# A long fused kernel on one core: taps copied straight from a row in SBUF, and a new order of the first loads, decodes and splits

## The chip, the cores and the metric

The kernel runs on 1 core of a Trainium2 chip. The metric is device time in microseconds (us) of one execution, the median of several runs; lower is better. Three runs of the kernel before took 1014.91, 1015.44 and 1015.61 us.

## The reference, cut to what matters

Three stages on x of shape (4, 4224, 192), everything float32. `weight` is 8 x 7, `U` is 4224 x 32, `V` is 32 x 4224, and each of the two MLPs has `w_ch1` of 192 x 768 and `w_ch2` of 768 x 192.

```python
# 1. causal convolution along the sequence: 7 taps (a softmax over weight), 8 heads of 24 channels
w = softmax(weight, axis=-1)
x = einsum('hk,bskhg->bshg', w, windows_of_7(x))
# 2. low-rank mixing along the sequence, then an MLP
u = x + ((x^T @ U) @ V)^T
x = u + relu(u @ w_ch1) @ w_ch2
# 3. real part of a 2-D Fourier transform, a normalization, then a second MLP
u = x + real(fft(fft(x, axis=1), axis=2))
out = u + relu(normalize(u) @ w_ch1') @ w_ch2'
```

On the host only the layout is changed; `U`, `V` and the MLP weights arrive as pairs of 32-bit words (float64 bits), which the kernel turns into float32 itself.

## The kernel before, in words

**Units of work.** The sequence of a batch is cut into 11 blocks of 384 rows. There are 88 block passes: 44 through the first MLP (stage 0), 44 through the second (stage 1). A pass has four pieces. The preparation (`pre1` for stage 0) adds the low-rank term to a block, takes its row sizes, makes the reciprocal scales (`scales`: tiles `cmax`, `rc`), splits the scaled block into a high and a low float16 part (`high` on ScalarE, `low` on GpSimd), and transposes both through a DMA into tile `ch`. `layer1` has six units, one per 128 hidden features: five matmuls of 384 columns, then an eviction by ScalarE (`hh`, line 650) and one by VectorE (`hl`, line 651). `layer2` has three units of 18 matmuls, closed by line 704; the result is stored to the DRAM tensor `x2d`.

**The start.** Before the first pass the kernel must make the first batch's convolution. `weight` is turned into taps on one partition (lines 983 to 989, tile `rowt`). The convolution's matrices are 64 shifted copies of that row per half of the partitions (tile `tap`); the row goes to the DRAM tensor `rowd` (lines 965, 966, 991) and comes back from there in two DMAs (line 995). x arrives in three chunks per batch (`load_x`, tiles `xw`, three buffers); the first two have 128 x 2688 floats, the third 128 x 1920. Each chunk is convolved by PE (line 398, 16 matmuls per pair of heads), evicted in place by ScalarE (line 404), stored to DRAM as `x1d` (line 368) and multiplied with U (`gunit`, line 414). After the third chunk the 32 x 192 product is replicated (`gfin`: matmul `gr`, tile `grep`), which every stage-0 block of batch 0 needs (line 522, tile `h`; added on VectorE by line 525).

**Decoding.** `decode` turns two words into one float32 with five VectorE instructions of up to 384 columns: line 172 takes off the sign bit, 175 clamps, 176 shifts, 178 and 179 put the words together. A decoded MLP weight also gets a largest value (line 223, tile `mx`). From `mx` the scale comes through a matmul (`all_max`, tile `am`, line 121), and then the weights are split into float16 high and low parts (`split1h`, `split1e`, `split1a`, `split1b` for the first layer, `split2` for the second; lines 257 and 264). The first MLP's raw weights arrive in three parts: `wa`, `wb` (first layer) and `wc` (second layer).

**What sets the order.** Everything is issued in program order, engine by engine; SP issues nearly all DMAs, in order, and an SP instruction that waits holds up all behind it. The order of the start is a table of strings, `START`: a letter with a number runs so many units of a queue (`c` first batch's convolution, `d` the second's, `w` the first MLP's weights, `a` and `b` the preparation of blocks 0 and 1, `z` later pieces of V, `e` the split of V). Other names are single jobs: `X`, `Y` load chunks of batch 0 and 1, `P` parts of the weights, `U1`, `V`, `V12` parts of U and V, `u`, `v0` decode them, `A0` and `s` store chunks of `x1d` (`A0` the first 448 rows), `L` loads a block, `S` loads `sel`, `B0` and `B1` are matmuls on zeros that give PE something to do (18 and 44 of them, `AGAIN`), after 52 at the very start (`WARM`). The first string runs before block 0; string t runs after two units of layer 1, three strings to a block. The table `windows` places the second MLP's weights and all else over later steps.

## Time and profile before

| | |
|---|---|
| runs | 1014.91, 1015.44, 1015.61 us (median 1015.44) |
| span of the profiled execution | 1017.3 us, 1.9 us above the median; no other time is listed for it |
| PE busy | 979.1 us, 96% of the span |
| VectorE, ScalarE, GpSimd busy | 748.4, 604.4, 380.9 us |
| HBM | 61.69 MB read, 46.11 MB written |

PE (TensorE) is busy nearly all the time, so what can be won or lost lies in the stretches in which it waits, or in which its granted clock is below 1.00. The page's busy shares are means over the whole span; the first 130 us differ from the rest, so the views that matter are those by stretch: the windows (busy time, granted clock and DMA rate of each stretch), the timeline (single instructions, with the idle time before them and what ended it) and the waits. A row of the windows has the stretch, its length, then for PE, weight loads (PEld), VectorE (DVE), ScalarE (ACT) and GpSimd (POOL) the busy us and the instructions that begin in it, then PE's granted clock, the DMA engines' share and GB/s. A row of the timeline has start and length in us (of a merged run, from its first start to its last end), engine, line, instruction, tiles, sizes and count, and in brackets the idle time just before.

### The profile page before, as it was taken

How to read it: one execution, taken by the hardware profiler on the slowest of the kernel's cores; microseconds unless marked ns; L12 is line 12 of the kernel's file. 1: busy time of each engine (PE TensorE's matmuls, PEld its weight loads, DVE VectorE, ACT ScalarE, POOL GpSimd, SP SyncE). 2: the span in 40 equal slices, each digit the busy share in tenths (PEclk: the TensorE clock that was granted, in tenths of full speed). 3: DMA queues.
4: the chain of work that ended last, by engine and by line, in shares of the span. 5: the costliest groups of instructions: out<-in, count | busy, mean ns of one | idle time of the engine just before them, and what ended most of it. 6: DMA issues, size and time to landing. Idle time of an engine off the chain costs nothing.

```text
span 1017.3 us, 25682 instructions
## 1 busy us (share of the span) xinstructions
PE 979.1 (96%) x9929; PEld 764.8 (75%) x9929; DVE 748.4 (74%) x2094; ACT 604.4 (59%) x1512; POOL 380.9 (37%) x397
## 2 busy tenths in 40 slices
PE   8789898999899999999999999998999999999998
PEld 5466676777677777877778887776888877877776
DVE  7766577689876656687776777897789787766663
ACT  2556554765676666656576666655656665555552
POOL 0111111253552344265534445564157651562110
PEclk9999999999999999999999999999999999999999
DMA  7596857685536666443425455433344332542332
GB/s 288 155 230 183 252 148 189 178 213 158 151 99 154 203 201 179 114 138 101 102 73 146 134 155 139 108 87 82 87 131 110 107 87 65 137 110 68 82 72 63
DMA packets 190804, 139.28 MB, mean 137 GB/s; under 512 B 128186, under 2 KB 164257, under 8 KB 189913
## 3 DMA queue, kind: packets, MB, share of 16 engines
q1 hardware_dynamic: 183095, 124.59, 45.6%
q0 software_dynamic: 7104, 12.70, 4.8%
q8 instruction: 77, 1.26, 0.5%
q14 instruction: 46, 0.38, 0.1%
q10 hardware_dynamic: 482, 0.35, 0.1%
HBM read 61.69 MB, written 46.11 MB: 106 GB/s over the span
## 4 chain that ended last, share of the span: by engine, by line
PE 62%; DVE 12%; DMA 11%; POOL 5%; issue 5%; ACT 4%; SPq 0%; DVEq 0%; ACTq 0%; POOLq 0%
PE l L665 24%; PE l L697 9%; PE l L701 8%; PE l L699 8%; PE l L655 5%; DMA ch<-sp 4%; DVE hl L651 3%; DMA xm<-x2d,mrow 2%; POOL xm L756 2%; PE cv L398 2%; PE sd L863 2%; PE s L879 2%; DMA x1d<-xw 1%; DVE x L790 1%; POOL xp L804 1%
## 5 line engine op out<-in xcount | busy, mean ns | idle before, releaser
L665 PE MATMUL l<-ch,w1h 128*128 128x384 f16 x1584 | 407.2, 327 | 15.4 <-DMA ch<-sp 10.1
L697 PE MATMUL l<-w2h,hh 128*128 128x192 f16 x1584 | 391.9, 247 | 5.8 <-DVE hl L651 4.5
L699 PE MATMUL l<-w2l,hh 128*128 128x192 f16 x1584 | 391.4, 247 | 1.2 <-DVE w2l L264 1.2
L701 PE MATMUL l<-w2h,hl 128*128 128x192 f16 x1584 | 391.4, 247 | 0.5 <-DVE hl L651 0.4
L651 DVE SCALAR_TENSOR_TENSOR hl<-l,hh 128x384 f16<-128x384 f32 x528 | 267.6, 549 | 127.2 <-ACT hh L650 126.1
L650 ACT ACTIVATE hh<-l 128x384 f16<-128x384 f32 x528 | 235.3, 494 | 155.7 <-PE l L655 155.3
L665 PEld LDWEIGHTS <-w1h 128*128 128x128 f16 x1584 | 155.1, 98 | 106.8 <-DMA ch<-sp 12.3
L697 PEld LDWEIGHTS <-hh 128*128 128x128 f16 x1584 | 155.6, 98 | 23.1 <-issue 12.3
L665 PE MATMUL l<-ch,w1l 128*128 128x384 f16 x528 | 172.7, 327 | 0.0
L699 PEld LDWEIGHTS <-hh 128*128 128x128 f16 x1584 | 155.7, 98 | 17.1 <-issue 6.5
L701 PEld LDWEIGHTS <-hl 128*128 128x128 f16 x1584 | 155.7, 98 | 3.1 <-DVE hl L651 1.4
L561 POOL TENSOR_TENSOR sp<-un,sp 128x576 f16<-128x576 f32 x44 | 57.3, 1302 | 250.4 <-ACT sp L578 228.3
L655 PE MATMUL l<-ch,w1l 128*128 128x384 f16 (+1 forms) x528 | 133.9, 327 | 0.0
L756 POOL DMA_INDIRECT xm<-x2d,mrow x84 | 84.9, 1011 | 21.3 <-issue 17.8
L631 POOL TENSOR_TENSOR sp<-un,sp 128x576 f16<-128x576 f32 x34 | 44.9, 1320 | 120.2 <-ACT sp L578 118.9
L625 ACT ACTIVATE un<-u,mr,rs 128x192 f32<-128x192 f32 x132 | 62.4, 537 | 25.3 <-DVE mr L619 24.7
L555 ACT ACTIVATE un<-u,rc 128x192 f32<-128x192 f32 x132 | 50.2, 445 | 43.0 <-DVE rc L550 43.0
L704 DVE SCALAR_TENSOR_TENSOR u<-l,cmax,u 128x192 f32<-128x192 f32 x132 | 54.5, 413 | 25.5 <-PE l L701 20.9
L665 PEld LDWEIGHTS <-w1l 128*128 128x128 f16 x528 | 51.8, 98 | 28.0 <-issue 4.0
L543 ACT ACTIVATE junk<-u 128x192 f16<-128x192 f32 x132 | 47.7, 361 | 40.6 <-DVE u L534 24.2
L849 POOL DMA_INDIRECT u<-x2d,mrow x64 | 62.4, 975 | 15.3 <-issue 11.7
L704 DVE SCALAR_TENSOR_TENSOR u<-l,ws,u 128x192 f32<-128x192 f32 x132 | 53.9, 410 | 18.2 <-PE l L701 18.0
(136 smaller groups left out, 1189.5 us busy)
## 6 DMA issues: line engine op xcount, KB each, us to landing
x2d<-u SPq DMA_DIRECT2D x68, 288.0 KB
u<-x1d SPq DMA_DIRECT2D x44, 288.0 KB
out_d<-u SPq DMA_DIRECT2D x43, 288.0 KB
x1d<-xw SPq DMA_DIRECT2D x36, 210.0 KB
u<-x2d SPq DMA_DIRECT2D x32, 192.0 KB
x<-x2d SPq DMA_DIRECT2D x60, 99.0 KB
xw<-x_d SPq DMA_DIRECT2D x4, 1344.0 KB
xw<-x_d SPq DMA_DIRECT2D x8, 672.0 KB
```

The costliest lines, as they stand in the source:

```text
L561: low_engine(0, b, j).tensor_tensor(out=sp[:, :, D:2 * D], in0=k["un"], in1=sp[:, :, :D], op=ALU.subtract)
L625: nc.scalar.activation(un[:, t], u[:, t], AF.Identity, scale=k["r"][:, t:t + 1], bias=k["m"][:, t:t + 1])
L650: nc.scalar.activation(hh[:, m], acc[m], AF.Relu)
L651: nc.vector.scalar_tensor_tensor(out=hl[:, m], in0=acc[m], scalar=0.0, in1=hh[:, m], op0=ALU.max, op1=ALU.subtract)
L655: nc.tensor.matmul(acc[m].rearrange("p (r n) -> p r n", r=TB), lhsT=w["l1"][rows, n, m * P:(m + 1) * P], rhs=kd[x][rows], start=False, sto ...
L665: nc.tensor.matmul(o, lhsT=w[v][:, e, ms], rhs=kd[x], start=(n == 0), stop=False)
L697: nc.tensor.matmul(o, lhsT=hh[:, m, rs], rhs=w["h2"][:, m], start=(m == 0), stop=False)
L699: nc.tensor.matmul(o, lhsT=hh[:, m, rs], rhs=w["l2"][:, m], start=False, stop=False)
L701: nc.tensor.matmul(o, lhsT=hl[:, m, rs], rhs=w["h2"][:, m], start=False, stop=(m == NM - 1))
L704: nc.vector.scalar_tensor_tensor(out=u[:, r], in0=o, scalar=sc, in1=u[:, r], op0=ALU.mult, op1=ALU.add)
L756: nc.gpsimd.indirect_dma_start(out=xs[c][1][:, g], out_offset=None, in_=x2d[b][:], in_offset=bass.IndirectOffsetOnAxis(ap=mrow[:99, k:k + ...
L849: nc.gpsimd.indirect_dma_start(out=u2[:, s0 + 2 * e], out_offset=None, in_=src[:], in_offset=bass.IndirectOffsetOnAxis(ap=mrow[:, k2 + e - ...
```

## The change

The taps no longer pass through DRAM: one VectorE memset clears a longer row, and two DMAs read the 64 shifted copies from that one row, which lies on one SBUF partition. `decode` has a new argument: for U's two halves and the first layer's weights (`wa`, `wb`) ScalarE takes the sign off by an Abs, instead of line 172 on VectorE; the scratch tile `dec` has two buffers. The order of loads, decodes, scales and splits in `START` is another, the matmuls on zeros are 34, 20 and 44, the store `A0` is issued by SP instead of ScalarE, and `split1a` stands ahead of `split1e`.

```diff
-WARM = 52
-AGAIN = (18, 44)
+WARM = 34
+AGAIN = (20, 44)
...
-        def decode(raw, out):
+        def decode(raw, out, first=False):
...
-            t = wrk.tile([P, DN], I32, name="dec", bufs=1)[:p, :n]
+            t = wrk.tile([P, DN], I32, name="dec", bufs=2)[:p, :n]
             g, h = nc.vector.tensor_scalar, nc.vector.scalar_tensor_tensor
-            g(out=t, in0=hi, scalar1=0x7FFFFFFF, scalar2=None, op0=ALU.bitwise_and)
-
             f = t.bitcast(F32)
+            if first:
+                nc.scalar.activation(f, hi.bitcast(F32), AF.Abs)
+            else:
+                g(out=t, in0=hi, scalar1=0x7FFFFFFF, scalar2=None, op0=ALU.bitwise_and)
...
-                decode(st["raw"][:, a:z], st["w"][:, a:z])
+                decode(st["raw"][:, a:z], st["w"][:, a:z], i == 0 and z <= FF + FH)
...
-                                       lambda: scaled(0, FF + FH, 0), split1h, split1e, split1a, split1b] + \
+                                       lambda: scaled(0, FF + FH, 0), split1h, split1a, split1e, split1b] + \
...
-        rowt = wrk.tile([1, KC * H], F32, name="hh", tag="hh")
+        rowt = wrk.tile([1, (2 * KC - 1) * H], F32, name="hh", tag="hh")
...
-        part(0)
+        load_x(0, 0)
         load_uv("u", 0, UH)
-        zer = wrk.tile([1, KC * H], F32, name="hl", tag="hl")
-        nc.vector.memset(zer, 0.0)
-        nc.scalar.dma_start(rowd[:, :nz], zer[:, :nz])
-        nc.scalar.dma_start(rowd[:, KC * H:], zer[:, :(KC - 1) * H])
+        nc.vector.memset(rowt, 0.0)
...
-        nc.sync.dma_start(rowd[:, nz:KC * H], rowt[:, nz:])
-
-        load_x(0, 0)
         for i in range(2):
-            nc.sync.dma_start(tap[KC * i:KC * i + KC].rearrange("p o h -> p (o h)"), bass.AP(
-                tensor=rowd.tensor, offset=rowd.offset, ap=[[H, KC], [1, KC * H]]))
+            nc.sync.dma_start(
+                tap[KC * i:KC * i + KC].rearrange("p o h -> p (o h)"),
+                bass.AP(tensor=rowt.tensor, offset=rowt.offset,
+                        ap=[list(rowt.ap[0]), [H, KC], [1, KC * H]]))
+        part(0)
...
-            decode(uv["u"][:, sl], uf[:, sl])
+            decode(uv["u"][:, sl], uf[:, sl], True)
...
-                    s0=lambda: stores[0](0, FIRST), A0=lambda: stores[0](0, 0, FIRST, nc.scalar))
+                    s0=lambda: stores[0](0, FIRST), A0=lambda: stores[0](0, 0, FIRST),
+                    L0=lambda: pre_load(0, 0))
...
-            "S U1 P1 X1 X2 V w2 u0 c4 B0 A0 L0 s0 L1 P2 u1 w c5 w3 v0 c4 w c3 w2 a4 w a4 b2 B1 w b4 w L2 b2 w",
-            "w s1", "", "w2 L3 V12", "w s2", "Y0", "z", "", "z", "d", "d Y1", "d", "d z", "d", "d z", "d Y2", "d e", "d", "d e", "d e",
+            "X1 U1 X2 S u0 w2 c4 A0 V P1 B0 L0 s0 P2 u1 c5 L1 s1 Y0 v0 c4 w c2 w3 c w a3 w a5 w2 B1 b4 w b4 w L2 w",
+            "w2", "", "w2 L3 V12", "s2", "Y1", "z", "", "z", "d", "d", "d z", "d", "d z Y2", "d", "d e", "d", "d e", "d", "d e",
```

Three places show how the instructions now stand (the lines of the code move by one or two). The first is VectorE behind the first layer's weights: `w1h` and `w1l` are their split parts, `cmax` and `rc` a block's scales, `u<-h,u` the low-rank addition (to block 0 first, then to block 1), `dec<-u` the first step of decoding `wc`. Before:

```order
L287 COPY w1h_90<-w1h_90 64x768
L525 TENSOR_TENSOR u<-h,u 128x192 x3
L294 COPY w1h_90<-w1h_90 64x384
L264 SCALAR_TENSOR_TENSOR w1l_91<-u_89,sc_370,w1h_90 64x384
L294 COPY w1h_90<-w1h_90 64x384
L264 SCALAR_TENSOR_TENSOR w1l_91<-u_89,sc_370,w1h_90 64x384
L296 COPY w1l_91<-w1l_91 64x768
L547 TENSOR_SCALAR cmax<-cmax 128x3
L550 RECIPROCAL rc<-cmax 128x3
L525 TENSOR_TENSOR u<-h,u 128x192 x3
L172 TENSOR_SCALAR dec<-u_89 128x384
```

And now:

```order
L287 COPY w1h_89<-w1h_89 64x768
L288 COPY w1h_89<-w1h_89 64x768
L548 TENSOR_SCALAR cmax<-cmax 128x3
L551 RECIPROCAL rc<-cmax 128x3
L295 COPY w1h_89<-w1h_89 64x384
L265 SCALAR_TENSOR_TENSOR w1l_90<-u_88,sc_435,w1h_89 64x384
L295 COPY w1h_89<-w1h_89 64x384
L265 SCALAR_TENSOR_TENSOR w1l_90<-u_88,sc_435,w1h_89 64x384
L297 COPY w1l_90<-w1l_90 64x768
L526 TENSOR_TENSOR u<-h,u 128x192 x3
L175 TENSOR_SCALAR dec<-u_88 128x384
```

Block 0's scales stand ahead of the split's last five instructions, no more behind them; block 0's addition, which stood among the splits, is now ahead of them all (just before these rows). Block 1's addition stands directly ahead of `wc`'s decoding in both.

The second is PE in block 0's layer 1, where `am` takes the largest value of `wc` to all partitions. `l_648` is the last of the six units before, `l_677` the first of block 1. Before:

```order
L655 LDWEIGHTS w1l_91
L655 MATMUL l_648<-ch,w1l_91 128x384
L121 MATMUL am<-sel,mx_94 128x128
L665 LDWEIGHTS w1h_90
L665 MATMUL l_677<-ch,w1h_90 128x384
L665 LDWEIGHTS w1l_91
L665 MATMUL l_677<-ch,w1l_91 128x384
```

And now, where `l_583` is block 0's second unit, `l_610` its third, and `h` the low-rank matmuls of block 2:

```order
L656 LDWEIGHTS w1l_90
L656 MATMUL l_583<-ch,w1l_90 128x384
L120 MATMUL am<-sel,mx_93 128x128
L523 MATMUL h<-grep,vt 128x192 x3
L666 LDWEIGHTS w1h_89
L666 MATMUL l_610<-ch,w1h_89 128x384
```

Four units of block 0 that stood ahead of `am` stand behind it. The 44 matmuls on zeros, which followed the `h` of blocks 0 and 1, now stand between the two.

The third is SP in block 4 (strings 13 to 15 and on), where batch 1's last chunk of x (`xw<-x_d` with 1920) goes past stores of its first chunk, and then the second MLP's first weights are loaded (`u_..<-wa_d`). Before:

```order
L585 DMA_TRANSPOSE ch<-sp 128x12x128
L504 DMA u<-x1d_66 128x576
L368 DMA x1d_67<-xw 56x5x192 x4
L368 DMA x1d_67<-xw 56x4x192 x2
L159 DMA xw<-x_d 128x1920
L716 DMA x2d_70<-u 128x576 x2
L585 DMA_TRANSPOSE ch<-sp 128x12x128
L504 DMA u<-x1d_66 128x576
L201 DMA u_1474<-wa_d 128x1536
```

And now:

```order
L586 DMA_TRANSPOSE ch<-sp 128x12x128
L505 DMA u<-x1d_66 128x576
L369 DMA x1d_67<-xw 56x5x192 x2
L158 DMA xw<-x_d 128x1920
L369 DMA x1d_67<-xw 56x5x192 x2
L369 DMA x1d_67<-xw 56x4x192 x2
L717 DMA x2d_70<-u 128x576 x2
L586 DMA_TRANSPOSE ch<-sp 128x12x128
L505 DMA u<-x1d_66 128x576
L202 DMA u_1453<-wa_d 128x1536
```

The load of the chunk stands ahead of four of the six stores `x1d<-xw`, no more behind them all; what follows, up to `wa_d`, is the same.

## Rows read from the trace of the kernel before

**Rows 1.** The page, its head.

```profile
span 1017.3 us, 25682 instructions
```

**Rows 2.** Windows of 20 us.

```profile
0.00:20.00 20.00, 17.60 (x134) 10.31 (x134) 14.94 (x40) 4.38 (x10) 1.41 (x7) 1.00 0.87 317
40.00:60.00 20.00, 13.51 (x87) 8.28 (x87) 17.06 (x45) 11.46 (x31) 2.56 (x2) 0.96 0.70 189
120.00:140.00 20.00, 16.63 (x178) 11.87 (x177) 13.84 (x39) 12.48 (x35) 2.81 (x3) 0.83 0.70 207
```

**Rows 3.** Timeline of PE at the start.

```profile
1.26 11.51 PE L975 MATMUL l<-hl 128*128 128x384 f16 x52 [1.26 <-POOL hl L970]
13.59 2.57 PE L398 MATMUL cv<-xw,tap 64*64 64x168 f32 x62 [0.33 <-DMA tap<-rowd]
```

**Rows 4.** Windows at the start.

```profile
0.00:10.00 10.00, 8.74 (x36) 4.53 (x37) 6.14 (x18) 1.53 (x2) 1.41 (x7) 1.00 0.78 274
11.00:12.00 1.00, 1.00 (x8) 0.61 (x7) 0.93 (x3) 0.00 (x0) 0.00 (x0) 1.00 0.70 144
15.00:16.00 1.00, 1.00 (x34) 0.91 (x26) 0.46 (x3) 1.00 (x4) 0.00 (x0) 1.00 1.06 447
```

**Rows 5.** Timeline of VectorE, decoding of U, then of wc.

```profile
14.62 0.39 DVE L179 SCALAR_TENSOR_TENSOR ut<-u,dec 128x224 int32<-128x224 int32 x1
39.67 0.36 DVE L172 TENSOR_SCALAR dec<-u 128x384 int32<-128x384 int32 x1 [3.44 <-DMA u<-wc_d]
42.04 0.55 DVE L223 TENSOR_REDUCE mx<-u 128x1 f32<-128x384 f32 x1
```

**Rows 6.** Timeline of ScalarE, 28 to 36 us.

```profile
28.10 1.09 ACT L257 ACTIVATE w1h<-u,sc 128x768 f16<-128x768 f32 x1
30.97 0.33 ACT L431 ACTIVATE grep<-gr 128x192 f32<-128x192 f32 x1 [1.78 <-PE gr L427]
32.51 0.36 ACT L543 ACTIVATE junk<-u 128x192 f16<-128x192 f32 x1
35.48 1.15 ACT L555 ACTIVATE un<-u,rc 128x192 f32<-128x192 f32 x3 [1.54 <-DVE rc L550]
```

**Rows 7.** Timeline of PE and VectorE, 32 to 66 us.

```profile
32.20 7.32 PE L975 MATMUL l<-hl 128*128 128x384 f16 x44
42.20 0.32 PE L665 MATMUL l<-ch,w1h 128*128 128x384 f16 x1 [2.67 <-DMA ch<-sp]
49.55 0.32 PE L665 MATMUL l<-ch,w1h 128*128 128x384 f16 x1 [2.49 <-DVE hl L651]
49.88 0.14 DVE L230 TENSOR_REDUCE mx<-mx 128x1 f32<-128x3 f32 x1
64.24 0.25 PE L701 MATMUL l<-w2h,hl 128*128 128x192 f16 x1
65.78 0.34 PE L665 MATMUL l<-ch,w1h 128*128 128x384 f16 x1 [1.30 <-DVE xmax L712]
```

**Rows 8.** Windows with a low clock.

```profile
59.00:60.00 1.00, 1.00 (x9) 0.94 (x8) 1.00 (x4) 0.97 (x5) 0.00 (x0) 0.50 0.93 305
126.00:128.00 2.00, 2.00 (x15) 1.58 (x15) 1.31 (x4) 1.78 (x4) 0.00 (x0) 0.50 0.96 183
```

**Rows 9.** Timeline of SP, VectorE and PE, 102 to 125 us.

```profile
102.18 0.42 SPq L159 DMA_DIRECT2D xw<-x_d  x1
112.51 0.43 SPq L201 DMA_DIRECT2D u<-wa_d  x1
117.57 0.26 DVE L172 TENSOR_SCALAR dec<-u 128x192 int32<-128x192 int32 x1 [3.41 <-DMA u<-wa_d]
124.86 0.32 PE L697 MATMUL l<-w2h,hh 128*128 128x192 f16 x1 [3.37 <-DVE hl L651]
```

**Rows 10.** Windows at 82 and 101 us, for the DMA rate.

```profile
82.00:83.00 1.00, 1.00 (x8) 0.61 (x7) 0.79 (x3) 0.17 (x1) 0.65 (x1) 1.00 1.19 408
101.00:102.00 1.00, 1.00 (x23) 0.82 (x16) 0.58 (x2) 1.00 (x5) 0.00 (x0) 1.00 0.89 282
```

More of the change, by code (lines that the diff above doesn't have):

```diff
@@ L159, in load_x @@
             nc.sync.dma_start(xw_t[b, c][:, ks], io["x"][b, c][:, ks])
-        def decode(raw, out):
+        def decode(raw, out, first=False):
             p, n = raw.shape[0], raw.shape[1]
             if n > DN:
-                decode(raw[:, :DN], out[:, :DN])
-                decode(raw[:, DN:], out[:, DN:])
+                decode(raw[:, :DN], out[:, :DN], first)
+                decode(raw[:, DN:], out[:, DN:], first)
                 return
             lo, hi = raw[:, :, 0], raw[:, :, 1]
-            t = wrk.tile([P, DN], I32, name="dec", bufs=1)[:p, :n]
+            t = wrk.tile([P, DN], I32, name="dec", bufs=2)[:p, :n]
             g, h = nc.vector.tensor_scalar, nc.vector.scalar_tensor_tensor
-            g(out=t, in0=hi, scalar1=0x7FFFFFFF, scalar2=None, op0=ALU.bitwise_and)
             f = t.bitcast(F32)
+            if first:
+                nc.scalar.activation(f, hi.bitcast(F32), AF.Abs)
+            else:
+                g(out=t, in0=hi, scalar1=0x7FFFFFFF, scalar2=None, op0=ALU.bitwise_and)
             g(out=f, in0=f, scalar1=W_MIN, scalar2=W_MAX, op0=ALU.max, op1=ALU.min)
@@ L954, in build @@
         nz = (KC - KW) * H
-        rowt = wrk.tile([1, KC * H], F32, name="hh", tag="hh")
-        row = rowt[:, nz:].rearrange("p (t h) -> p h t", h=H)
+        rowt = wrk.tile([1, (2 * KC - 1) * H], F32, name="hh", tag="hh")
+        row = rowt[:, nz:KC * H].rearrange("p (t h) -> p h t", h=H)
         UH = UC * R // 2
@@ L1013, in build @@
                     U1=lambda: load_uv("u", UH, 2 * UH),
[L1014 removed]
+                    s0=lambda: stores[0](0, FIRST), A0=lambda: stores[0](0, 0, FIRST),
+                    L0=lambda: pre_load(0, 0))
         for n in range(4):
             jobs.update({f"X{n}": lambda n=n: load_x(0, n), f"Y{n}": lambda n=n: load_x(1, n),
[L1017 removed]
+                         f"P{n}": lambda n=n: part(n), f"L{n + 1}": lambda n=n: ahead_load(n + 1),
                          f"s{n + 1}": lambda n=n: stores[0](n + 1),                          f"u{n}": lambda n=n: dec_u(n)})
```

2 lines of the change are left out of this document (removed).

## The prediction, made before the changed kernel had run

> **What bounds the kernel now.** The span is 1017.3 us [rows 1], and over most of it PE is busy without a break, so I first read the windows of 20 us for the stretches where it is not. Three stand out early [rows 2]: PE is busy 17.6 of 20 us at the start (most of it on zeros), 13.5 of 20 from 40 to 60 us, and 16.6 from 120 to 140, where the granted clock is 0.83 as well. All edits fall before 135 us. Behind that the order is the same, so what is won or lost up to there moves the rest in time, and I take it to come out at the end one for one.
>
> Then the timeline, for what each stretch waits on. At the start PE runs its 52 matmuls on zeros to 12.8 us and begins the convolution in earnest at 13.59, released by the taps' DMA [rows 3]. Layer 1 of block 0 begins at 42.20 after a wait for the transposed block, stops until 49.55 because VectorE, which is decoding `wc`, frees no PSUM [rows 7], and layer 2 of block 0 runs in part at clock 0.50, 1.2 GHz of 2.4 [rows 8]; it ends at 64.5, and block 2 begins at 65.78 [rows 7]. Later VectorE waits 3.41 us for the second MLP's `wa`; what it holds up makes PE wait 3.37 us at 124.86 [rows 9], and PE goes on at clock 0.50 to about 130 [rows 8]. So there are two places to price: the start up to 65 us, and the one at 112 to 130 us.
>
> **The start, step by step.**
>
> *Loads.* The first chunk of x (128 x 2688 floats, 1.38 MB) and half of U (0.62 MB) now go first; `wa` (0.79 MB) goes behind the taps. At the 274 GB/s of the first ten us [rows 4] U's half is through by about 7.5 us and, with 1.6 us for landing, there at 9.0 (the taps of before ended 3.05 MB of bytes, through at about 11.9 us by the rates of [rows 4], and let PE go at 13.59 [rows 3]). The taps (two times 64 rows of 2 KB, 0.26 MB) have 0.79 MB less ahead of them: 2.9 us, so 10.7 instead of 13.6. Their own price is not in the trace, since nothing there reads one partition for many. Bounds: 1.8 us at the 144 GB/s that the DMAs moved while the old taps passed [rows 4]; and, if one partition gives no more than one of the 16 DMA engines takes (447 / 16 = 28 GB/s [rows 4]), 9.4 us. Zero is excluded, the bytes are the same. I take 1.8, from the row of the same bytes to the same partitions, and keep 9.4 for a rival. The zeros end in time: 18 fewer at 7.32 / 44 = 0.166 us [rows 7] is 3.0 us less, so at 9.8. `wa` is then there at 12.4, the second chunk at about 16.
>
> The Trainium skill, "SBUF — State Buffer", section "Door 1: The DMA port swizzle", says that four partitions hang on one DMA port of about 27 GB/s. By that, as an estimate, the taps would take 9.6 us; no run so far shows it.
>
> *VectorE up to `grep`.* A decoded piece of 384 columns takes 2.37 us and 0.55 for its largest value (39.67 to 42.59 [rows 5]); the first instruction, now ScalarE's, is 0.40 of that. A piece of 224 columns costs 0.39 / 0.56 = 0.7 of it. The Abs is new: between 0.36 us (Abs of 192 columns) and 1.09 (768 columns) [rows 6], by columns 0.6. Most hide beside VectorE's work, since `dec` has two buffers; the first (after U lands) and `wb`'s (behind the third chunk's evictions) do not. So from 9.6: U 3.35, `wa` two times 2.55, U 3.35, the copy of `gacc` 0.4, V's first piece 2.4, the wait for an Abs 0.6, `wb` 2.55, two additions 0.8 = 28.1. VectorE, not PE, is now the bound here: the old order reached this point through the taps, three stages of convolution and `gacc`. Largest value, `am`, reciprocal: 1.45. `grep` starts at 29.6 instead of 30.97 [rows 6]: 1.3 won. Seven removed instructions of VectorE are worth 2.5 us of this.
>
> *From `grep` to layer 1.* On ScalarE `w1h` (1.09) comes first, then the three sizes (1.65 with their read-outs). VectorE has `w1l` 1.0 and two copies 0.75 to do before the scales (0.4): un at 33.35 instead of 35.48 [rows 6]. The way from there to the first matmul stays 6.7 us: 40.1 instead of 42.20 [rows 7], 2.1 won.
>
> *`wc`.* It is issued behind the first store and no more behind block 1's load, and lands near 31 us instead of 39.67. That buys little, since its decoding stands behind block 1's addition, that one behind block 1's `h`, and `h` now behind the 44 zeros: 30.5 + 7.3 + 0.3, then the addition 0.9, so 39.0. From there to the end of `mx` VectorE has what it had before, 10.3 us (39.67 to 50.0 [rows 5, 7]): 49.3. Of the 2.1 us, 0.7 is left here.
>
> *PE behind `am`.* PE does two units (five matmuls of 0.166, 0.83 each) to 41.8 and then stands at `am`, to 49.8. That is the new wait, 8 us; before, five units had gone ahead of it. Then ten units 8.3 and two `h` 1.1: 59.2. An idle time of 3.37 us was followed by 5.3 us at clock 0.50 [rows 8, 9], so the clock will fall here too; 3.4 to 5.3 us at half speed lose 1.7 to 2.6, I take 2.2: 61.4. Layer 2 of block 0, 54 matmuls of 0.083, ends at 65.9. `w2l`, for which PE waited before, is made earlier and hidden. Before it was 64.5: **the start loses 1.4 us**, though its first half wins 2.1.
>
> *Moves at no price.* `A0` on SP waits for the first chunk's evictions (to 16.6); behind it are V's first piece, `wb` and the stores. V is needed at 21.9 and would be there at 21.5; if it is later, VectorE waits by that much. Batch 1's first chunk goes before the first transpose instead of at 63 us; its bytes are through by 37.8, just before the transpose's. PE's two more zeros fill a wait for x.
>
> **The second place.** Batch 1's last chunk (0.98 MB) was issued at 102.18 [rows 9], behind six stores, right ahead of the store of `x2d` whose landing lets SP go on to `wa` at 112.51 [rows 9]. Now it goes four stores (3.2 us) earlier. While only stores run, the DMAs move 282 GB/s, with a load of x among the work 408 [rows 10]: 126 GB/s for 3.2 us is 0.40 MB, 1.4 us at 282. Bounds: 0, if the stores are held up by as much, and 3.2. V's scale (three VectorE instructions, 0.65 with the gaps) now stands ahead of the wait, not behind it. The wait of PE shrinks from 3.37 to 1.3. Waits of 2.67 and 2.49 us [rows 7] did not lower the clock: the 0.96 of 40 to 60 us [rows 2] is used up by the low windows from 58 on [rows 8]. So I let the clock stay, which gives back 2.6 of the 5.3 us. **Won: 2.0 + 2.6 = 4.6 us.**
>
> **Sum.** +1.4 - 4.6 = -3.2 us on a profiled span of 1017.3, which lies 1.9 above the median of the runs; taken from the median, 1015.4 - 3.2 = **1012.2 us**. A difference under 0.2%, 2.0 us, can't be told from no change.
>
> **The rivals.**
>
> *The taps choke the queue (slower).* All copies come from one partition; if that gives 28 GB/s, every load behind them is 7.6 us later. VectorE's work on U covers half a us of that, so the start is 7.1 worse: 1019.3, and 1023.9 if the second place is not won either. It decides from taps that take about 5.5 us. Against it: no row shows a single-partition limit. For it: none shows the contrary, and the page cited above speaks for it. Chance 0.22.
>
> *The second place stays.* All bytes between the transposes of blocks 4 and 5 are the same and only their order moves; if stores and load share the DMAs evenly, `wa` lands as late as before and the clock falls again. Then only the start counts: 1016.8. Chance 0.22.
>
> *The start keeps what it wins.* If PE's later units are covered by VectorE's evictions, which end 0.7 us earlier, and the clock costs no more than before, the start wins up to 2.1 instead of losing 1.4: 1008.7. Against it: ten units are 8.3 us, and the evictions are not longer. Chance 0.14.
>
> **Numbers.** The forecast has 0.42, with its own range 1010 to 1015. The range of 8 in 10 reaches from 1007.5 (the third rival) to 1020 (the first, with the second place won). Faster by over 2.0 us: 0.29 of the forecast, 0.14 of the third rival, 0.03 and 0.02 of the others, 0.48. Slower: 0.18 of the first rival, 0.08 of the second, 0.01 of the forecast, 0.27. The rest, 0.25, is within.
>
> **What would show it.** The first convolution matmul near 10.7 us (near 18 with the first rival); `grep` near 29.6; block 0's layer 1 near 40.1; then PE idle about 8 us until `am` near 49.8, and a clock of 0.50 behind it; layer 2 of block 0 ending near 66. Later `wa` landing about 1.4 us sooner after the chunk's stores, PE's wait there near 1.3 us and a clock of 1.00 from 120 to 140 us. I am wrong if the taps land after 14 us, if PE passes `am` without a long wait, or if the clock still falls at 124 us.

## The result, and the profile after

The changed kernel took 1028.22, 1029.11, 1029.79 and 1031.33 us (median 1029.45), the kernel before 1014.91 to 1015.61 (median 1015.24 of four runs): ratio 1.0123, interval 1.0088 to 1.0158. It is slower, outside the range given. In a second comparison, among the experiments below, the ratio was 1.0085 (1.0067 to 1.0103). In some comparisons below the kernel before itself takes about 1030 us and in others about 1017, on one and the same chip too, and the difference comes between 440 and 880 us, so a time is held only against that of the kernel before in the same comparison.

The profiled execution's own time is 1029.11 us, its span 1027.3; before the span was 1017.3 [rows 1], so 10.0 us more. In every run that lists both, the span is about 1.8 us below the time. By that, as an estimate, the profiled execution of before took 1019.1 us, 3.9 above the median of 1015.24, and not 1.9: of the 14.2 us between the medians, the two profiles can show 10.0. The page now begins:

```profile
span 1027.3 us, 25651 instructions
```

The windows of 20 us, to be held against [rows 2], show where it lies:

```profile
0.00:20.00 20.00, 13.74 (x98) 8.26 (x98) 7.15 (x20) 5.13 (x12) 1.41 (x7) 0.85 0.88 238
20.00:40.00 20.00, 17.29 (x245) 11.56 (x243) 14.26 (x37) 9.95 (x30) 0.00 (x0) 0.84 0.97 321
40.00:60.00 20.00, 10.57 (x61) 5.96 (x59) 14.44 (x38) 6.96 (x18) 2.55 (x2) 0.76 0.51 137
120.00:140.00 20.00, 18.61 (x225) 14.36 (x224) 13.58 (x40) 10.32 (x32) 1.79 (x3) 1.00 0.90 268
```

In the first 20 us PE is busy for 13.74 us, before 17.60, at a clock of 0.85, and VectorE does half of what it did (7.15 us, before 14.94). From 20 to 40 us the clock is 0.84, and from 40 to 60 us PE has lost another 2.9 us and a fifth of its clock. The last row is the other way round: from 120 to 140 us PE is busy for 18.61 us, before 16.63, and the clock stays at 1.00. So in this profile the start was lost and the second place won.

The start, timeline of PE (to be held against [rows 3]):

```profile
1.26 8.64 PE L973 MATMUL l<-hl 128*128 128x384 f16 x34 [1.26 <-POOL hl L968]
11.77 0.53 PE L399 MATMUL cv<-xw,tap 64*64 64x168 f32 x2 [1.86 <-DMA tap<-hh]
15.43 4.76 PE L399 MATMUL cv<-xw,tap 64*64 64x168 f32 x62 [3.14 <-DMA tap<-hh]
```

The taps come in two steps, the second half lets PE go at 15.43, and the convolution's 62 matmuls take 4.76 us at a clock that has meanwhile fallen, not 2.57. The windows of one microsecond show the DMAs at that time (the last two numbers are the DMA engines' share and GB/s):

```profile
5.00:6.00 1.00, 1.00 (x4) 0.45 (x3) 0.00 (x0) 0.00 (x0) 0.00 (x0) 1.00 0.96 401
8.00:9.00 1.00, 1.00 (x8) 0.61 (x7) 0.05 (x1) 0.63 (x2) 0.00 (x0) 1.00 1.08 35
11.00:12.00 1.00, 0.23 (x2) 0.27 (x2) 0.90 (x4) 0.00 (x0) 0.00 (x0) 1.00 0.76 23
15.00:16.00 1.00, 0.57 (x8) 0.56 (x12) 0.00 (x0) 0.00 (x0) 0.00 (x0) 0.50 1.03 435
```

While the taps pass, from 8 to 13 us, the DMAs move 23 to 35 GB/s, and still the mean share of the 16 reads 0.76 to 1.08. The trace has each DMA packet's time: the taps' 128 packets of 2 KB lie between 7.0 and 14.9 us and take 1.06 us each in the median. In the kernel before they take 0.11 us, between 9.4 and 13.1 us. `wa` was issued right behind, at 5.05 us, and its first packet comes at 13.16. Its timeline on ScalarE and VectorE (to be held against [rows 5, 6]):

```profile
17.25 1.01 ACT L173 ACTIVATE dec<-u 128x384 f32<-128x384 f32 x2 [8.03 <-DMA u<-wa_d]
36.14 0.33 ACT L432 ACTIVATE grep<-gr 128x192 f32<-128x192 f32 x1 [4.89 <-PE gr L428]
40.60 1.15 ACT L556 ACTIVATE un<-u,rc 128x192 f32<-128x192 f32 x3 [1.21 <-DVE rc L551]
43.02 0.97 DVE L295 COPY w1h<-w1h 64x384 f16<-64x384 f16 x1 [2.46 <-ACT w1h L258]
48.07 0.35 DVE L175 TENSOR_SCALAR dec<-u 128x384 int32<-128x384 int32 x1
```

`wa` is decoded from 17.25 us, `grep` comes at 36.14 (before 30.97), and `wc`, the last row, from 48.07 (before 39.67). PE then stands for it, timeline of PE (against [rows 7]), and a window of one microsecond behind it:

```profile
47.72 0.32 PE L666 MATMUL l<-ch,w1h 128*128 128x384 f16 x1 [0.47 <-DMA ch<-sp]
58.46 0.80 PE L120 MATMUL am<-sel,mx 128*128 128x128 f32 x2 [8.96 <-DVE mx L231]
74.88 0.34 PE L666 MATMUL l<-ch,w1h 128*128 128x384 f16 x1 [0.51 <-DVE cmax L692]
```

```profile
60.00:61.00 1.00, 1.00 (x6) 0.43 (x4) 0.80 (x4) 0.00 (x0) 0.00 (x0) 0.50 0.97 289
```

Layer 1 of block 0 begins 5.5 us late, PE stands 8.96 us at `am`, the clock is at 0.50 behind it until about 62 us, and block 2 begins at 74.88, before 65.78: **9.1 us lost.** Later, at the second place (against [rows 9]):

```profile
125.22 0.26 DVE L175 TENSOR_SCALAR dec<-u 128x192 int32<-128x192 int32 x1 [1.48 <-DMA u<-wa_d]
131.94 0.24 PE L698 MATMUL l<-w2h,hh 128*128 128x192 f16 x1 [1.18 <-DVE hl L652]
```

VectorE waits 1.48 us for `wa`, before 3.41; PE waits 1.18, before 3.37.

To follow the loss from there I read SP's 88 transposes, one per block, in the timeline. The sixth was issued at 95.04 before and at 104.14 now (+9.10), the eleventh at 165.52 and 170.86 (+5.34): **3.8 us won.** Then +6.39 at the 31st, +6.96 at the 81st, +8.78 at the last, and 10.0 at the end: what was won at the second place is lost again in small pieces.

### The profile page after: what moved, and what is told of

Same layout as the page of the kernel before. It is cut to its first block, busy times and chain, and to the rows that moved or that the text cites. A ratio compares the mean times of both kernels' runs of the same rounds, so it can differ in the third digit from the quotient of the medians.

```text
span 1027.3 us, 25651 instructions
## 1 busy us (share of the span) xinstructions
PE 981.5 (96%) x9913; PEld 765.0 (74%) x9913; DVE 747.0 (73%) x2087; ACT 607.8 (59%) x1519; POOL 379.6 (37%) x397
## 4 chain that ended last, share of the span: by engine, by line
PE 65%; DVE 11%; DMA 10%; issue 5%; POOL 4%; ACT 4%; SPq 1%; DVEq 0%; ACTq 0%; POOLq 0%
PE l L666 25%; PE l L698 8%; PE l L702 8%; PE l L700 8%; PE l L656 5%; DMA ch<-sp 5%; DVE hl L652 4%; PE cv L399 3%; PE sd L864 2%; DMA xm<-x2d,mrow 2%; PE gp L415 1%; POOL xm L757 1%; PE s L824 1%; PE s L880 1%; PE l L973 1%
```

## The experiments

The time of the kernel before in the same comparison stands in brackets. For the stretches I use the sixth and the eleventh transposes, whose differences to the profile of before show the start, and the start with the second place. They come from one profile of each kernel. The five kernels that leave the start nearly as it was stand at -0.7 to -1.7 us at the sixth transpose, so the profile of before is itself about 1 us late there.

| run | what is in it | median us (before) | ratio, interval | 6th, us | 11th, us |
|---|---|---|---|---|---|
| the change | | 1029.45 (1015.24) | 1.0123, 1.0088 to 1.0158 | +9.1 | +5.3 |
| v4_change | the change again | 1039.24 (1030.58) | 1.0085, 1.0067 to 1.0103 | +6.9 | +4.9 |
| t1_taps_dram | change, taps through DRAM | 1025.74 (1017.74) | 1.0070, 1.0044 to 1.0097 | +6.8 | +3.5 |
| t3_am_late | change, `am` behind six units | 1025.87 (1017.74) | 1.0079, 1.0051 to 1.0108 | +3.3 | +0.2 |
| t4_dram_am_late | both | 1022.31 (1017.74) | 1.0044, 1.0028 to 1.0060 | -0.5 | -2.1 |
| v1_dram_am_y0 | both, and batch 1's chunk late | 1033.47 (1030.58) | 1.0036, 1.0022 to 1.0051 | -1.2 | -3.2 |
| w3_old_compute | these three, old scales and splits | 1027.47 (1030.17) | 0.9991, 0.9966 to 1.0016 | -3.0 | -5.8 |
| x2_a0_back | the same, `A0` by ScalarE | 1018.43 (1019.18) | 0.9999, 0.9986 to 1.0012 | -2.5 | -5.8 |
| v3_wa_first | change, `wa` ahead of taps | 1042.06 (1030.58) | 1.0105, 1.0080 to 1.0130 | +9.9 | +9.1 |
| w1_half_copied | change, half the taps from the row | 1039.72 (1030.17) | 1.0102, 1.0074 to 1.0130 | +11.8 | +8.3 |
| t2_row_only | before, taps from the row | 1020.50 (1017.74) | 1.0022, 1.0006 to 1.0039 | +2.4 | +0.6 |
| w2_abs_alone | before, signs by ScalarE | 1030.00 (1030.17) | 0.9996, 0.9981 to 1.0012 | -1.0 | -1.0 |
| v2_second_place | before, second place | 1030.18 (1030.58) | 0.9982, 0.9965 to 0.9998 | -1.2 | -2.6 |
| x1_a0_on_sp | before, `A0` by SP | 1017.41 (1019.18) | 0.9986, 0.9972 to 1.0000 | -0.9 | -3.5 |
| w4_place_and_wc | before, second place, `wc` early | 1028.45 (1030.17) | 0.9980, 0.9962 to 0.9998 | -0.7 | -3.6 |
| y1_three_parts | before, these two and `A0` by SP | 1014.92 (1017.51) | 0.9978, 0.9957 to 0.9999 | -1.7 | -4.3 |

**The change again,** to have it beside others:

> The change itself, unaltered, beside the other three and the kernel before, so that they stand in one comparison. 1.0 to 1.4% over the kernel before.

It is slower by 0.85%, less than expected, and its sixth transpose comes 2.2 us earlier than in the first profile of the same program. PE's timeline differs too:

```profile
49.51 0.48 PE L666 MATMUL l<-ch,w1h 128*128 128x384 f16 x1 [4.54 <-DMA ch<-sp]
56.19 0.75 PE L120 MATMUL am<-sel,mx 128*128 128x128 f32 x2 [3.32 <-DVE mx L231]
```

Here PE waits 4.54 us for the transposed block and only 3.32 at `am`, where the first profile had 0.47 and 8.96.

**The taps and `am`, each undone and both.** The first:

```diff
+    rowd = drm.tile([1, (2 * KC - 1) * H], F32, name="rowd")
+        nc.sync.dma_start(rowd, rowt)
...
-                bass.AP(tensor=rowt.tensor, offset=rowt.offset,
-                        ap=[list(rowt.ap[0]), [H, KC], [1, KC * H]]))
+                bass.AP(tensor=rowd.tensor, offset=rowd.offset, ap=[[H, KC], [1, KC * H]]))
```

> The change with the taps' row written to DRAM once and read back from there, all else as in the change. If the taps' source is what cost the start (theory A): first convolution matmul at 10 to 11.5 us instead of 11.8 and 15.4, wa lands near 12.5 instead of 17.25, grep near 30, block 2 begins 6 to 7 us earlier than in the change (near 68), and the whole takes 1021 to 1024 us; the stand of PE at am stays, 8 to 9 us. If the order alone is at fault (theory B: the taps are hidden beside VectorE's work on U and the wait at am takes up the rest): 1028 to 1031 us, the same as the change. By the sum on record (taps at 1.8 us): 1012 us.

The second:

```diff
-            "w2", "", "w2 L3 V12", "s2", "Y1",
+            "w", "", "w2 L3 V12", "w s2", "Y1",
```

> The change with the scale of the second layer's weights (matmul am) behind six units of block 0 as before the change, and no more behind two; the taps stay as in the change. Theory A (PE stands at am for want of other work, and the idle time lowers the clock): four units, 3.3 us, go into the stand, the clock does not fall behind it or less, block 2 begins 3.3 to 5.5 us earlier: 1024 to 1026 us. Rival (PE's units need VectorE for their evictions, and VectorE decodes wc all that time, so PE stops for PSUM instead): under 1.5 us, 1028 to 1029.5 us.

> Both of these: taps through DRAM and am behind six units. If the two losses add (theory A): 9 to 12 us under the change, 1017 to 1020 us; if the sum on record was right in all but these two, block 2 begins near 64 and the whole takes 1009 to 1012 us. Rival (the two hide each other, since VectorE's decoding of wc sets the end of the start in any case): no better than the better of the two alone.

With the taps through DRAM, PE's timeline has:

```profile
11.73 3.92 PE L400 MATMUL cv<-xw,tap 64*64 64x168 f32 x62 [0.37 <-DMA tap<-rowd]
45.50 0.32 PE L667 MATMUL l<-ch,w1h 128*128 128x384 f16 x1 [2.84 <-DMA ch<-sp]
53.88 0.79 PE L121 MATMUL am<-sel,mx 128*128 128x128 f32 x2 [6.59 <-DVE mx L232]
71.90 0.34 PE L667 MATMUL l<-ch,w1h 128*128 128x384 f16 x1 [0.52 <-DVE cmax L693]
```

The taps are there at 11.73, `wa` at 14.13 (SP now stands 3.7 us for the row's way through DRAM before it can issue the taps and `wa`), `grep` at 31.71, 4.4 us earlier than in the change, and `am` passes 4.6 us earlier; but layer 1 begins only 2.2 earlier, since it now waits 2.84 us for its transposed block, the clock stays at 0.50 until about 60 us, and block 2 begins 3.0 earlier. So the run lies between the two theories, and the start is still 6.8 us late with the taps mended. With `am` late the stand at `am` is gone, and another has come:

```profile
50.17 0.48 PE L666 MATMUL l<-ch,w1h 128*128 128x384 f16 x1 [6.37 <-DMA ch<-sp]
```

The sixth transpose is 5.8 us earlier all the same, 3.7 against the change's second profile; and this profile is the fastest of its five runs (1021.53 us, median 1025.87). Both together make 9.6 us, 104.14 to 94.58, or 7.4 against the second profile. The start is level with before (theory A of both), but the whole, 1022.31 us, is still 0.44% slower, not within the 1017 to 1020 of theory A, and the same wait is there:

```profile
32.61 3.28 SPq L159 DMA_DIRECT2D xw<-x_d  x1
38.55 11.51 SPq L587 DMA_TRANSPOSE ch<-sp  x2
46.55 0.48 PE L667 MATMUL l<-ch,w1h 128*128 128x384 f16 x1 [6.58 <-DMA ch<-sp]
```

SP issues batch 1's first chunk (1.38 MB), then the transpose at 38.55; PE goes on 8.0 us later. Before, it took 3.4 us, to 42.20 [rows 7]:

```profile
38.79 1.42 SPq L585 DMA_TRANSPOSE ch<-sp  x1
```

So that load, too, seems not to be free; the next run tests it.

**Batch 1's chunks back at their old places.**

```diff
-            "X1 U1 X2 S u0 w2 c4 A0 V P1 B0 L0 s0 P2 u1 c5 L1 s1 Y0 v0 c4 ...
+            "X1 U1 X2 S u0 w2 c4 A0 V P1 B0 L0 s0 P2 u1 c5 L1 s1 v0 c4 ...
-            "w", "", "w2 L3 V12", "w s2", "Y1", "z", "", "z", "d", "d", "d z",
+            "w", "", "w2 L3 V12", "w s2", "Y0", "z", "", "z", "d", "d Y1", "d z",
```

> The change with three parts undone: taps through DRAM, am behind six units, and batch 1's first two chunks of x loaded where they stood before (block 1's first half and block 3), no more ahead of the first transpose. Theory A (in the run without the last of these, the first transpose landed 8 us after its issue and PE waited 6.58 us for it, with the chunk's load ahead of it in the queue; before it was 3.4): layer 1 of block 0 begins near 42 instead of 46.55, block 2 3 to 4.5 us earlier, the whole 0.25 to 0.45% less than with the two parts undone, so level with the kernel before or up to 0.1% under it. Rival (the transpose is late by its own work, or PE then stands for VectorE's decoding of wc as long): within 0.1% of the run with two parts undone, 0.3 to 0.5% above the kernel before.

Timeline of VectorE and PE:

```profile
37.62 0.97 DVE L296 COPY w1h<-w1h 64x384 f16<-64x384 f16 x1 [2.46 <-ACT w1h L259]
...
41.27 0.35 DVE L176 TENSOR_SCALAR dec<-u 128x384 int32<-128x384 int32 x1
...
42.89 0.32 PE L667 MATMUL l<-ch,w1h 128*128 128x384 f16 x1 [2.97 <-DMA ch<-sp]
```

Layer 1 begins 3.7 us earlier, at 42.89, so the load was what held the transpose; the sixth transpose gains only 0.8 of it. What sets the rest is in the other rows: VectorE waits 2.46 us for `w1h`, because ScalarE now does `un` and `sp` ahead of `w1h`'s halves, and comes to `wc` at 41.27, later than the 39.67 of before, without a wait for `wc` itself.

**The old order of scales, splits and zeros,** with these three undone:

```diff
-                                       lambda: scaled(0, FF + FH, 0), split1h, split1a, split1e, split1b] + \
+                                       lambda: scaled(0, FF + FH, 0), split1h, split1e, split1a, split1b] + \
-            "... c4 w c2 w3 c w a3 w a5 w2 B1 b4 w b4 w L2 w",
+            "... c4 w c2 w3 c w a w2 a3 w a4 b2 B1 w b4 w L2 b2 w",
```

> The change with the taps through DRAM, batch 1's first two chunks of x at their old places, and all of block 0's and 1's scales, splits, zeros and am in the old order; what is left of the change is the order of the first loads, wc ahead of block 1's load, ScalarE's signs, and the second place. Theory A (in the run with block 1's h behind the 44 zeros and the scales ahead of the splits, VectorE waited 2.46 us for w1h and came to wc at 41.3; before it was 39.67, and wc itself is there at 32): VectorE begins wc at 36 to 37, am passes 3 us earlier, layer 1 at 41.5 to 42.5, no stop in block 0, block 2 3 to 5 us earlier than before the change, the whole 0.4 to 0.8% under the kernel before. Rival (PE's own work and the transposes set block 2's start, VectorE does not): block 2 within 1.5 us of the kernel before, the whole within 0.25% of it.

VectorE begins `wc` at 39.03, 2.2 us earlier than in the last run, but not at 36 to 37, and layer 1 begins at 45.30, not at 41.5 to 42.5; the sixth transpose comes 3.0 us earlier than before, the eleventh 5.8. The whole is level with the kernel before (0.9991, interval 0.9966 to 1.0016): neither 0.4% nor a loss. What cost the change its start has now been taken out piece by piece: the sixth transpose stands at +9.1, +6.8, -0.5, -1.2 and -3.0 us, in single profiles, against a profile of before that is itself about 1 us late there.

**The taps from the row, alone,** in the kernel before:

```diff
-        nc.sync.dma_start(rowd[:, nz:KC * H], rowt[:, nz:])
...
-            nc.sync.dma_start(tap[KC * i:KC * i + KC].rearrange("p o h -> p (o h)"), bass.AP(
-                tensor=rowd.tensor, offset=rowd.offset, ap=[[H, KC], [1, KC * H]]))
+            nc.sync.dma_start(
+                tap[KC * i:KC * i + KC].rearrange("p o h -> p (o h)"),
+                bass.AP(tensor=rowt.tensor, offset=rowt.offset,
+                        ap=[list(rowt.ap[0]), [H, KC], [1, KC * H]]))
```

> The kernel before with one thing changed: both tap copies read the row on one SBUF partition, at the place where the DRAM copies stood. Theory A (one partition gives about 25 GB/s, so 0.26 MB take 10 us and hold up the loads behind them): the second half of the taps lands 7 to 8 us later than 13.6, the second chunk of x as well, the zeros end at 12.8 and PE stands and loses clock; block 2 begins 6 to 8 us later, 1021 to 1024 us. Rival (the taps' price is no more than through DRAM, what cost the start is the new order): 1013 to 1016 us.

A window, then PE's timeline:

```profile
11.00:12.00 1.00, 0.34 (x3) 0.00 (x0) 0.93 (x4) 0.00 (x0) 0.00 (x0) 1.00 0.94 29
```

```profile
16.87 4.67 PE L397 MATMUL cv<-xw,tap 64*64 64x168 f32 x62 [3.43 <-DMA tap<-hh]
```

From 10 to 14 us the same 25 to 31 GB/s, the same clock loss in the convolution; the second half lets PE go 3.3 us later than the taps before, not 7 to 8. Part of that is won by the way that falls away: SP issues the copies at 3.80 us, before, with the row going through DRAM, at 6.60. `grep` is 4.2 us late, block 2 2.6, the whole 0.22% (0.06 to 0.39): between theory and rival.

**`wa` ahead of the taps, and half the taps from the row.** The first:

```diff
+        part(0)
         for i in range(2):
             nc.sync.dma_start(
...
-        part(0)
```

The second, in place of the second of the two copies from the row:

```diff
+        nc.gpsimd.dma_start(tap[KC:2 * KC], tap[:KC])
```

> The change with wa issued ahead of the two tap copies instead of behind them. Theory A (what the slow taps cost is the wait for wa, 17.25 us, behind which VectorE stood 5.6 us): wa lands near 11 to 12, VectorE does not stand, grep 2 to 4 us earlier, though the taps end 2 us later (17.5); 2 to 3 us under the change at block 2. Rival (the convolution, not wa, sets the way to grep): grep no earlier or up to 2 us later, the whole level with the change or slower.

> The change with half as many bytes read from the one partition: the first tap copy as in the change, the second copies the first's 64 partitions, issued by GpSimd's queue. Theory A (one partition gives 25 GB/s to all readers, 5.2 us per copy, and the loads behind it in the queue wait): the first copy lands by 10.5 to 11.8, the second 2 to 3 us behind it, wa near 12.5 to 13.5 instead of 17.25, grep 3 to 4.5 us earlier than in the change. At block 2, where the wait for VectorE's decoding of wc takes part of it back, 2 to 4 us; the whole 0.2 to 0.4% under the change. Rival (the number of descriptors or the source's kind sets the time, not the partition): the second copy takes as long as the first, 15 us, and grep is level with the change.

In both theory A misses, and the first is near its rival. With `wa` first VectorE decodes it from 11 us on without a wait, but the taps let PE go only at 16.84, and ScalarE's order shows what then holds:

```profile
20.86 0.80 ACT L405 ACTIVATE xw<-cv 128x336 f32<-128x336 f32 x2
21.52 0.88 ACT L173 ACTIVATE dec<-u 128x384 f32<-128x384 f32 x2
```

U's second half, for which VectorE waits 4.89 us, has its signs taken off by ScalarE, and that stands behind the first chunk's eight evictions, which wait for the taps. `grep` is 35.66, level with the change. With half the bytes from the row, the rows of PE and VectorE are:

```profile
17.70 2.53 PE L399 MATMUL cv<-xw,tap 64*64 64x168 f32 x32 [6.32 <-DMA tap<-tap]
...
13.09 0.36 DVE L176 TENSOR_SCALAR dec<-dec 128x384 f32<-128x384 f32 x1 [0.95 <-ACT dec L173]
23.76 0.36 DVE L176 TENSOR_SCALAR dec<-dec 128x384 f32<-128x384 f32 x1 [5.63 <-ACT dec L173]
```

`wa` is decoded from 13.09, in the change from 17.84: half the bytes from one partition, 4.7 us less, as theory A has it. But GpSimd's copy, issued beside `wa` and x's second chunk (2.2 MB), let PE go only at 17.70, and the same Abs behind the evictions costs 5.63; `grep` comes at 38.52, 2.4 us later than in the change. So the taps hurt in two ways, through `wa` and through the convolution, and a cure of one is not enough.

**Signs by ScalarE, alone:** `decode` with the argument `first`, the Abs and two buffers of `dec`, as in the change's diff, in the kernel before.

> The kernel before with one thing changed: ScalarE takes the signs off U, wa and wb, with two buffers of dec. Theory A (before, grep is reached through taps, three stages of the convolution and gacc, not through VectorE): grep within 0.5 us of 30.97, block 2 within 1 us, the whole within 0.1%. Rival 1 (VectorE's seven instructions count here too): 1 to 2.5 us faster. Rival 2 (the two buffers move the other tiles, and that is what makes the transposes of the last blocks late by 1 us in three places in every run with the new order): level up to block 70, then 2 us slower.

0.9996 (0.9981 to 1.0012): theory A; no rival.

**The second place, alone.**

```diff
-... "d Y1", "d", "d z", "d", "d z", "d Y2", "d e", "d", "d e", "d e",
+... "d Y1", "d z", "d", "d z Y2", "d", "d e", "d", "d e", "d", "d e",
```

> The kernel before with one thing changed: batch 1's last chunk is loaded ahead of four of the six stores, and the units of V around it stand as in the change. Theory A (the wait of VectorE for wa at 117 us shrinks and the clock does not fall behind it): 3.5 to 4.6 us under the kernel before, 0.35 to 0.45% faster, granted clock 1.00 from 120 to 140 us. Rival 1 (what the change won there came from the state it arrived in): within 0.1%. Rival 2 (it is won there and lost again in later waits): block 11 some 3 us earlier, the end no more than 1.5.

With it `wc` ahead of block 1's load:

```diff
-            "S U1 P1 X1 X2 V w2 u0 c4 B0 A0 L0 s0 L1 P2 u1 w c5 ...
+            "S U1 P1 X1 X2 V w2 u0 c4 B0 A0 L0 s0 P2 L1 u1 w c5 ...
```

> The kernel before with two parts of the change alone: the second place, and wc issued ahead of block 1's load. Theory A: wc lands near 32 instead of 39.67, VectorE's idle 3.44 us goes, PE's stop of 2.49 us in block 0 and its waits for w2h and w2l (1.8 us) shrink, block 2 begins 2.5 to 4.3 us earlier; the whole 0.35 to 0.65% under the kernel before. Rival (block 1's load, now behind wc in the queue, makes block 1 late by as much): block 2 within 1 us of before, the whole within 0.1% of the run with the second place alone, 0.1 to 0.3% under the kernel before.

The first won 0.18%, half of what was expected; at the eleventh transpose it is 2.6 us early, at the 19th 1.0 (rival 2). With `wc` early the eleventh is 3.6 us early, block 2 begins 1.8 us earlier than before, and the whole is the same 0.20% (the rival).

**`A0` by SP, alone and taken back.** These two runs were to find the late loss: from the 81st transpose to the last all kernels with the change's first order of loads lose 1.4 to 2.1 us, those with the old order 0.2 at most. PE's timeline of `t4_dram_am_late`, then of `t2_row_only`, at one of the places:

```profile
963.66 0.34 PE L667 MATMUL l<-ch,w1h 128*128 128x384 f16 x1 [1.22 <-DMA ch<-sp]
```

```profile
964.18 0.34 PE L664 MATMUL l<-ch,w1h 128*128 128x384 f16 x1 [0.38 <-DMA ch<-sp]
```

The edit is one line, in the kernel before; the second run takes it back in `w3_old_compute`:

```diff
-                    s0=lambda: stores[0](0, FIRST), A0=lambda: stores[0](0, 0, FIRST, nc.scalar))
+                    s0=lambda: stores[0](0, FIRST), A0=lambda: stores[0](0, 0, FIRST))
```

> The kernel before with one thing changed: the store of the first 448 rows (A0) is issued by SP instead of ScalarE. It asks where the late loss comes from: in every run with the change's first order of loads the transposes of three blocks between 930 and 985 us end about 1 us later (2 us together), in none with the old order. Theory A (which queue's turn a transfer gets is set by how many each queue has had, and A0's move shifts that): start within 0.5 us, then the same 2 us lost at the end, the whole 0.15 to 0.25% over the kernel before. Rival (A0's queue has nothing to do with it): level all the way, within 0.1%.

> The run with the old order of scales, splits and am, taps through DRAM and batch 1's chunks at their old places, and now A0 by ScalarE again. Theory A: as that run up to block 70, then the 2 us at the end are not lost; 0.2 to 0.5% under the kernel before. Rival: ScalarE's queue now holds its next Abs behind the store's issue, grep 0.5 to 1.5 us later, and the end loses its 2 us all the same; within 0.15% of the kernel before.

`A0`'s move makes no late loss (0.0 from the 81st to the last), and taking it back does not mend it (1.4): not `A0`. Alone it stands 0.14% (0 to 0.28) under the kernel before, where its rival expected nothing and theory A a loss; with that interval it can't be told from no change. At the second place it is early all the same. VectorE there in `x1_a0_on_sp` (timeline), and the window behind it:

```profile
115.59 0.26 DVE L172 TENSOR_SCALAR dec<-u 128x192 int32<-128x192 int32 x1 [2.34 <-DMA u<-wa_d]
```

```profile
126.00:128.00 2.00, 1.79 (x22) 1.45 (x19) 1.89 (x4) 0.00 (x0) 0.26 (x1) 1.00 0.97 256
```

The same two in `w2_abs_alone`, which is level with the kernel before:

```profile
116.41 0.26 DVE L176 TENSOR_SCALAR dec<-u 128x192 int32<-128x192 int32 x1 [3.21 <-DMA u<-wa_d]
```

```profile
126.00:128.00 2.00, 2.00 (x19) 1.23 (x21) 1.33 (x1) 0.64 (x1) 0.26 (x1) 0.50 1.03 213
```

In `v2_second_place` the wait is 2.47 us, and the clock, 0.50 from 124 to 126, is back at 0.88 in this window. So in these runs a wait of 2.3 to 2.5 us goes with a clock that holds or is soon back, and one of 3.2 with a clock that stays down past 128 us. Two other runs do not fit. `t2_row_only` has the old order, ScalarE's `A0` and a wait of 2.38 us, and its clock falls; `v1_dram_am_y0` waits 3.30 us, and its clock stays at 1.00. The window behind the wait, of the first and then of the second:

```profile
128.00:130.00 2.00, 2.00 (x22) 1.25 (x23) 1.31 (x3) 1.20 (x2) 0.00 (x0) 0.50 1.13 189
```

```profile
124.00:126.00 2.00, 2.00 (x32) 1.62 (x33) 1.70 (x4) 2.00 (x5) 0.00 (x0) 1.00 1.12 72
```

Nor does the order of the stores alone set the wait: with the old order it is 2.34 to 3.41 us in four profiles, with the new one 1.48 to 3.68 in thirteen.

**All parts with a gain, together:** the kernel before with the edits of `w4_place_and_wc` and `x1_a0_on_sp`.

> The kernel before with three parts of the change and no other: the second place, wc issued ahead of block 1's load, and A0 issued by SP. Theory A (each took 0.14 to 0.20% off by itself or together, and two of them in different stretches): VectorE waits for wa at 112 to 118 us 2.0 us or less, the granted clock stays at 1.00 from 118 to 130 us, block 11 some 3.5 to 5 us earlier, of which 1.5 to 3 are given back behind it; the whole 0.2 to 0.45% under the kernel before. Rival (all three win at the same place, the clock behind 118 us, which can be won but once): no more than the 0.14 to 0.20% of each alone.

0.9978 (0.9957 to 0.9999), 1014.92 us beside 1017.51: the lowest ratio of all, but not to be told from the 0.9980 and 0.9982 above, so little or nothing more than each part alone, as the rival has it. Its wait for `wa` is 2.42 us, its clock 1.00 there, and its eleventh transpose 4.3 us early.

## Why the prediction was wrong

The direction was wrong, and the first rival came true in its mechanism: the taps choked the queue. Its time, 1019.3 us, was still 10 too low. Of the other two, the third fell, since the start kept nothing of its wins; the second, a second place that stays as it was, fell in the first profile and came half true in the second (`v4_change`).

- **The taps.** The step that failed is "I take 1.8, from the row of the same bytes to the same partitions". What that row had not in common was the source. From one partition the DMAs moved 23 to 35 GB/s, and the packets took 7.9 us from the first to the last; of the two bounds the other, 28 GB/s and 9.4 us, was the near one. The taps were complete at 15.43 us instead of 10.7, and `wa` was decoded from 17.25 instead of 12.4. The Trainium skill, "SBUF — State Buffer", section "Door 1: The DMA port swizzle", gives one port about 27 GB/s; by that, the trace agrees.
- **What the taps do not explain.** The rival's 7.1 us beside the forecast's start are close to what came, 9.1 instead of 1.4, but in part by luck: `t1_taps_dram`, with the taps mended, is still 6.8 us late there, and `t2_row_only`, which has only the taps from the row, with `wa` ahead of them, loses 2.4 us there, or 3.1 to 4.1 beside the five kernels with nearly the old start. Three other steps failed at the start, the next one and those on batch 1's chunk and `wc`.
- **The clock ahead of `am`.** `grep` came at 36.14 instead of 29.6, 6.5 late. From `grep` to `wc`'s decoding it was 11.9 us instead of 9.4, so `am` passed at 58.46 instead of 49.8. Of these 2.5 us, 1.9 are the 44 zeros, for which I took the 7.32 us of [rows 7]. With VectorE as the bound, PE waits for the first layer's `am`, whose `mx` VectorE ends at 34.60: 0.57 us before, 2.3 to 2.5 in all ten profiles with the change's order of first loads. I put that wait and its clock at nothing. In six of the ten profiles the zeros behind it took 8.8 to 9.3 us, in four 7.32, as with the old order. That is the clock of 0.84 from 20 to 40 us. Timeline of PE, before and then now, and the wait of VectorE ahead of `wc`:

```profile
24.87 0.46 PE L121 MATMUL am<-sel,mx 128*128 128x128 f32 x2 [0.57 <-issue]
```

```profile
37.47 9.24 PE L973 MATMUL l<-hl 128*128 128x384 f16 x44
47.27 0.89 DVE L526 TENSOR_TENSOR u<-h,u 128x192 f32<-128x192 f32 x3 [1.42 <-PE h L523]
```

- **How it went on.** From `am` to the end of block 0's layer 2 it was 15.9 us, predicted 16.1, in both profiles of the change. The stand of 8 us came in the first (8.96); in the second it was 3.32 behind a wait of 4.54 for the transposed block, so the agreement is in part luck.
- **"Moves at no price"** failed for batch 1's chunk. Its bytes were to be through just before the transpose; with `am` late and the taps mended the transpose came while they still passed, and PE waited 6.6 us; with the load at its old place it waited 3.0. In the change's first profile this is hidden (0.47 us), because the transpose is late anyway; in its second PE waits 4.54 us.
- **`wc` from 39.0** failed by an omission: with the scales ahead of the splits, ScalarE's `un` and `sp` come ahead of `w1h`'s halves, and VectorE waits about 2.46 us for these in all runs with that order. I had followed VectorE's queue there and not ScalarE's. Where the zeros take 7.32 us this shows: 10.1 us from `grep` to `wc` in three runs, not 9.4. In the change itself the wait for block 1's `h` behind the slow zeros ends later and covers it.
- **`am` ahead of four units** was seen, but its price was set against a gain in the first half which never came. Undone, it gives back 5.8 us at the sixth transpose against the change's first profile and 3.7 against its second; the taps give back 2.3 and 0.1, or 3.7 with `am` mended. By the whole times (1.0079 and 1.0070) the two can't be told apart, so which cost more is not shown. A late start and a stand hide each other in part.
- **The second place** was won in the first profile, 3.8 us of 4.6; in the second profile of the same program it was 2.0, with a wait of 2.45 us for `wa` and a clock of 0.50 from 132 to 134 us. That the price lies in the clock fits: it fell behind the wait in the kernel before and in `w2_abs_alone`, and held in the change's first profile. But what the clock does is not settled by the length of the wait (2.38 us lost it, 3.30 kept it), and that the new order is what shortens the wait is not shown. What speaks for the order are the ratios of `v2_second_place` and `w4_place_and_wc`, 0.9982 and 0.9980, whose intervals reach 0.9998.
- **"One for one" at the end** failed too. From the eleventh transpose to the 19th every run loses, the change 0.9 us and the others 0.4 to 5.3, in part in waits for a transposed block (in the change 2.28 us for one at 176 us, before 1.18); and near the end, from the 81st to the last, the change loses another 1.8. This second loss is there in all ten profiles with the change's first order of loads (1.4 to 2.1 us) and in none of the six with the old one (0.2 at most). It is not `A0`, not ScalarE's signs with their two buffers, not the second place, not the taps' row and not `wc` ahead of block 1's load. Which other part of that order it is was not tried.

In sum, in the spans of the two profiles: 9.1 us lost at the start, 3.8 won, 4.7 lost in pieces behind it, 10.0 in all. The other 4.2 us between the medians no profile shows.

## What to carry to other kernels

Price a transfer by its source as well as its bytes: here 128 reads of one partition went at 23 to 35 GB/s, and the load queued behind them waited as long. Where an operation moves to another engine or another place in an order, follow that engine's queue, not only the one it left; here the signs hung on the convolution's evictions and the splits on ScalarE's `un`. And when a start has several engines that end close together, undo the parts one after the other and together: alone they gave back 2.3 and 5.8 us, together 9.6, since the next wait is ready. And profile a program twice before a stand in one trace is called its cost.
